# A new hand-written order and engine choice for the first 1086 recorded operations of a fused SSM-convolution and gMLP block

## The chip, the cores and the metric

The kernel runs on one core of a Trainium2 chip. A core has five engines that each work through their own instructions in order and wait for one another by semaphores: TensorE (PE in the profile), VectorE (DVE), ScalarE (ACT), GpSimd (POOL) and SyncE (SP), which here issues nearly all DMAs. The metric is the device time of one execution, in microseconds.

## The reference, cut to what matters

Batch 1, sequence S = 2048, width D = 640, F = 1728 with Fh = 864. Block A is a short convolution of `k` times `v`, a long convolution of the result with `ssm_k` by FFT, and a gate with the normalized input; block B is a gMLP that mixes along the sequence. Both are modulated by `silu(c) @ w_mod`.

```python
mod = (_silu(c) @ w_mod).reshape(c.shape[0], 6, 1, -1)     # sa, ca, ga, sb, cb, gb
h = _layernorm(x, axis=-1) * (1 + ca) + sa                 # x = A_q
# block A
k_shift = sum over 4 taps of k_pad[:, t:t+S, :] * shift_k[:, 3 - t]
kv = k_shift * v
y = irfft2(rfft2(kv padded to 2S) * rfft2(ssm_k padded to 2S))[:, :S]
y = y + kv * ssm_D
x = x + ga * (h * y)
# block B
h = _layernorm(x, axis=-1) * (1 + cb) + sb
z = gelu(h @ w_in)
z1, z2 = z[..., :Fh], _layernorm(z[..., Fh:], axis=-1)
g = einsum('ts,bsf->btf', w_sp, z2) + b_sp[None, :, None]
x = x + gb * ((z1 * g) @ w_out)
```

## The kernel before, in words

**What sets the order.** Everything up to the mix's first tile pair is recorded in a list of 1086 operations (class `Plan`); an operation is one closure that emits from one to some twenty instructions, or one DMA. The string `ORDER` (from L40) lists them as an engine letter and an operation number: P for PE, D for DVE, A for ACT, G for POOL, S for a DMA issued by SP. `Plan.run` emits them in that order. The letter decides which engine computes the operation where its closure allows more than one. Each engine then runs its own instructions strictly in the order in which the string names them, so an instruction whose input isn't there holds up all behind it on that engine. Tiles come from rotating pools; a tile's next user waits until the last reader of the buffer is through, so the list also sets how far one engine may run ahead of another. At most eight of SP's DMAs are under way at a time. Behind the plan, a plain loop over the tile pairs 1 to 7 and the last projection follow.

**The stages, by the names in the profile.**

- *Start.* `k` and `v` are brought in transposed by DMA (L521, into `big`), in halves for the first 128 channels. The four taps are matmuls of `big` with diagonal weights `dg` (built from `ident` and `sk` at L536 or L538, ahead of which `sk` is turned by PE), into the PSUM tile `sm`; DVE multiplies by `v` (L553) and SP writes the product `kv` to the DRAM scratch `kv_scr` (L559), from which it is read back in the order that the transform wants (L390, `X<-kv_scr`). `ssm_k` is read straight into `X` (L390); DVE adds `ssm_D` to its first row (L400). Tables of cosines are made: `T` (DVE, L343 and L345), `M` (ACT's sine at L348, the sign at L353, the negative at L356), `G` (PE flips of `M`, copies at L248, negatives at L375), `F1bd` (L255 and L300).
- *Transform, five groups u of 128 channels.* Stage 1 (`X` with `F1bd`, PSUM copied out by L248), then eight steps a group: forward matmuls into `pu` for `ssm_k` (copied to `KH` by ACT) and for `kv`; the **product** of the two by DVE (L462, 40 of these, into `Tf` or `T`); for half of the steps two sums into `W` (L476, by POOL or DVE); inverse matmuls into `pz`, copied to `Z` by ACT or DVE (L248). `Z` is turned by DMA (L685) or, for u = 4, by PE, and the last matmuls give `y`.
- *First norm and gate.* The statistics of the 16 token tiles of `xt` (loaded in four DMAs of four tiles, L566) are taken by ACT (L576, L577: two passes with accumulation, written to `gh`) or by DVE (L580, L581); L590 to L592 finish ACT's share; L606, L608 or L610 write the normalized `gh`. The gate (L661, L678, L746), the residual (L698) and the second norm's statistics (L704) come per group.
- *Second norm and first gMLP matmul.* In four groups g of four token tiles: variance (L829), `rstd` (POOL, L190 and L191), `nmr` (L833), the normalized tile `Z` (L843, L845 or L847). For g = 0 PE turns `Z` in two pieces (L858) and DVE or ACT modulate it (L871, L869); for g = 1 to 3 SP turns it by a DMA transpose (L889) and L895 or L897 modulate. Then come 64 **zz** groups, each of five matmuls of 432 columns into `pz` or `pu`; ACT's gelu (L920) writes each out, DVE takes statistics of one half (L926).
- *Mix.* Weight tiles `wT` (L974), sums `S` and `T` (L988, L998) and the products (L1013) of a Strassen-like scheme on pairs of token tiles; `w_o` (L1074, seven DMAs) and `bsp` (L1066, one DMA) are loaded for it. The first pair belongs to the plan.

Six groups of **fills** (L245 with `ident`, no useful result) keep PE at work in its first microseconds.

The lines that set the order:

```python
        for e, i in order:
            o = self.ops[i]
            assert e in o["eng"] and done.issuperset(o["deps"]), (e, i)
            ...
            o["fn"](engines[e])
            done.add(i)
```

Of the kernel before, what the change touches and what calls it, by code (L numbers as in the profile page):

```python
# [54 lines left out]
P313 A557 A314 P309 P331 A332 P61 D652 S94 D96 G298 D563 D564 G655 A310 P67 D62 P311 P375 D68 A312 P349 D350 P333 D334
P289 G597 D670 P73 A376 A558 A559 A560 P343 D344 P77 G598 P377 P317 A318 D129 A290 P277 A278 G335 D595 D596 A378 D653
G336 P323 A324 P299 D592 P337 A300 P319 A320 A338 G345 S71 D78 S599 G346 D74 D616 P379 A380 P369 G713 P600 G612 S69
P351 A352 P279 P347 D370 D601 P381 A382 P602 D280 D603 P365 P79 D366 D80 A348 G654 P604 P383 A384 S95 P399 A400 D605
P387 A388 P359 G281 G282 P283 A284 G371 G372 P401 A402 D360 P606 D607 G613 P353 D354 S97 P385 A386 D99 S580 D618 P403
A404 P75 P397 A398 P395 A396 D619 D671 P405 A406 P373 A374 P339 G361 G362 P363 A364 D615 P449 A450 G608 D76 P413 P367  # L60
A368 G355 D340 D414 P407 D408 P341 A342 G617 P453 G709 S620 P621 D622 G674 P393 D650 A454 P389 A394 A390 S81 G356 P623
D624 P451 A452 P439 D440 P357 A358 P625 D626 P391 A392 P455 P427 G409 G410 P627 P417 G609 P581 G673 G656 D428 G429
D430 A456 S98 P411 A412 D418 P471 A472 P473 D628 A474 D634 P431 P457 G419 G420 P443 P479 A458 D444 A480 D629 D632 P467
A468 P421 A432 P423 D424 G445 P475 A476 P433 D434 A582 S657 G639 A422 P415 G676 P461 A462 D631 P477 A478 D630 D638
P463 A464 P658 D659 A416 P465 A466 P441 A442 G446 P660 D635 P481 G435 P447 A448 P497 G710 D661 P662 G436 P437 A438
P425 A426 D482 D663 P664 D498 S583 P517 D518 G677 G483 G484 P485 A486 P507 D508 P499 P459 A460 P469 P501 A470 D665
G675 G519 G520 P521 A522 G509 G510 A500 A132 G708 P487 P584 D502 P513 D488 P511 A512 P491 P489 G503 A490 D514 P515
G504 D492 S678 G668 P505 P679 A516 A506 G493 D494 P495 A585 D633 D680 P681 D682 A496 P719 A720 D636 S586 P683 D684
P715 P721 A722 D716 P685 D686 D687 P717 A718 P587 A588 P723 P726 P725 G666 D691 G711 D689 D688 P724 D727 G714 G692
D728 D729 D758 D730 D759 G760 D690 D731 D732 D734 P735 P1037 D772 P1036 D761 A762 P749 D736 D750 D737 P589 S756 D741  # L70
D740 G763 P764 D766 D767 D768 S757 A590 G667 G610 D696 P765 A769 P742 D733 D738 D693 D834 D771 A770 D637 P794 G773
D695 D836 P812 P784 A795 A813 D751 D754 D774 P818 D837 P791 A775 D739 D694 D835 G697 D698 D776 P778 G838 A819 D839
A785 A840 D842 G843 P777 A782 A783 P787 A788 P816 A817 D780 G712 D841 P814 A815 D640 A792 D779 D781 P808 A809 D796
D752 P822 A823 S844 P820 A821 P824 A825 A846 P798 A848 D743 D789 D702 G669 D703 D706 G845 D744 D745 D746 D900 P801
D611 A799 D644 S1038 P805 A806 D793 P826 A802 A827 D641 D699 D901 D847 G849 P850 A851 D797 P857 P867 A868 D747 P892
A893 D643 D701 D755 D748 P882 D903 S1039 A883 D700 D642 D902 A858 P874 A875 D647 P880 G904 D905 D906 G908 D786 D907
D909 S910 D810 A881 P890 A891 P860 G915 A861 P864 A865 G911 P871 A872 P884 D1054 D1055 D1057 D705 D968 A912 D1056 D807
D811 G913 A885 D648 D704 D753 D645 D966 D646 D967 D969 G970 D866 P888 A889 S1040 D859 D862 D863 P886 A914 P878 A887
# [7 lines left out]
A1071 P1074 D1078 D1082 P1076 D1075 D1079 S1080 P1083 P1018 A1019 P1022 P1010 A1023 D1084 S1085 A1011 D1060 D1061
P1016 A1017 D1047 D1051 D1052 D1050
"""


# [1215 lines left out]
```

## Time and profile before

| | us |
|---|---|
| three runs | 308.17, 309.71, 309.59 |
| their median | 309.59 |
| the profiled execution | 310.85 |
| its span, first to last instruction | 309.1 |
| PE busy (share of the span) | 293.9 (95%) |
| DVE busy | 270.7 (88%) |
| POOL busy | 181.2 (59%) |
| ACT busy | 166.6 (54%) |

The span is what the rows of the profile add up to; 1.75 us lie around it in the profiled execution. That execution is 1.26 us above the median of the three runs. Where a row says `L580 DVE BATCH_NORM_STATS2 st<-xt 128x6 f32<-128x320 bf16 x16 | 6.9, 472 | 1.0 <-...`, it gives line, engine, operation, the tile written and the tile read with their partitions and elements, the count, the busy time of all in us, the mean of one in ns, and the engine's idle time just before them with what ended it. The granted TensorE clock is full in all 40 slices of the page. Rows of PE overlap a little, since the matmuls are pipelined and their ends are modelled.

### The profile page before, as it was taken

How to read it: one execution, taken by the hardware profiler on the slowest of the kernel's cores; microseconds unless marked ns; L12 is line 12 of the kernel's file. 1: busy time of each engine (PE TensorE's matmuls, PEld its weight loads, DVE VectorE, ACT ScalarE, POOL GpSimd, SP SyncE). 2: the span in 40 equal slices, each digit the busy share in tenths (PEclk: the TensorE clock that was granted, in tenths of full speed). 3: DMA queues.
4: the chain of work that ended last, by engine and by line, in shares of the span. 5: the costliest groups of instructions: out<-in, count | busy, mean ns of one | idle time of the engine just before them, and what ended most of it. 6: DMA issues, size and time to landing. Idle time of an engine off the chain costs nothing.

```text
span 309.1 us, 6509 instructions
## 1 busy us (share of the span) xinstructions
PE 293.9 (95%) x2485; PEld 195.3 (63%) x2485; DVE 270.7 (88%) x523; ACT 166.6 (54%) x302; POOL 181.2 (59%) x208
## 2 busy tenths in 40 slices
PE   7988989989999998989999999999999999999995
PEld 2765678867889998645555555555555555565554
DVE  8898998979998988998897998998999878888574
ACT  6988699978888957547676688141111111021110
POOL 2542877838988999555423612039858475673922
PEclk9999999999999999999999999999999999999999
DMA  8999899998995849404679910073477593730323
GB/s 177 210 227 253 231 305 224 220 190 196 225 223 113 203 84 298 152 2 95 127 146 237 204 3 0 2 127 70 89 152 165 120 192 73 167 81 21 83 55 111
DMA packets 127954, 45.23 MB, mean 146 GB/s; under 512 B 117071, under 2 KB 127156, under 8 KB 127924
## 3 DMA queue, kind: packets, MB, share of 16 engines
q1 hardware_dynamic: 127770, 44.78, 68.1%
q8 instruction: 19, 0.31, 0.4%
q14 instruction: 11, 0.09, 0.1%
q10 hardware_dynamic: 154, 0.05, 0.1%
HBM read 16.11 MB, written 5.24 MB: 69 GB/s over the span
## 4 chain that ended last, share of the span: by engine, by line
PE 47%; DVE 12%; issue 1%; POOL 1%; DMA 1%; ACT 1%; DVEq 0%; POOLq 0%
PE ps L1013 21%; PE pu L245 8%; PE pz L245 8%; PE po L1179 6%; DVE st L704 2%; PE pz L1013 1%; PE po L1140 1%; DVE Tf L462 1%; DMA uT<-u 1%; DVE T L462 1%; DVE xt L698 1%; PE pu L1013 1%; DVE u L1041 1%; DVE T L998 1%; DVE gh L746 1%
## 5 line engine op out<-in xcount | busy, mean ns | idle before, releaser
L245 PEld LDWEIGHTS <-Z 128*128 128x128 bf16 x320 | 31.2, 98 | 28.1 <-DVE Z L871 1.3
L245 PE MATMUL pu<-X,M 128*128 128x128 bf16 (+1 forms) x480 | 45.8, 237 | 2.3 <-DVE Tf L462 1.9
L245 PEld LDWEIGHTS <-M 128*128 128x128 bf16 x480 | 37.4, 98 | 8.8 <-issue 3.2
L476 POOL TENSOR_TENSOR W<-Tf 128x256 bf16<-128x256 f32 x47 | 34.7, 760 | 11.6 <-DVE Tf L462 8.3
L1013 PEld LDWEIGHTS <-S 128*128 128x128 bf16 x256 | 25.0, 98 | 21.6 <-issue 0.5
L245 PE MATMUL pz<-big,Z 128*128 128x432 bf16 x160 | 33.1, 346 | 0.8 <-DVE Z L871 0.8
L248 ACT CAST X<-s 128x1024 bf16<-128x1024 f32 x31 | 31.9, 1028 | 2.5 <-PE s L245 2.3
L245 PE MATMUL pu<-big,Z 128*128 128x432 bf16 x160 | 32.5, 346 | 0.0
L462 DVE TENSOR_TENSOR Tf<-pu,KH 128x1024 f32<-128x1024 f32 x25 | 30.3, 1219 | 2.4 <-PE pu L245 1.2
L1197 ACT COPY O<-po 128x320 f32<-128x320 f32 x7 | 3.0, 427 | 54.4 <-PE po L1179 54.4
L1013 PEld LDWEIGHTS <-wT 128*128 128x128 bf16 x192 | 18.8, 98 | 16.6 <-issue 1.0
L245 PEld LDWEIGHTS <-G 128*128 128x128 bf16 x330 | 24.7, 98 | 2.0 <-issue 0.2
L248 ACT CAST KH<-pu 128x512 bf16<-128x512 f32 x40 | 23.0, 600 | 5.1 <-PE pu L245 5.1
L248 ACT CAST Z<-pz 128x512 bf16<-128x512 f32 x38 | 22.3, 601 | 5.3 <-PE pz L245 5.1
L245 PEld LDWEIGHTS <-X 128*128 128x128 bf16 x288 | 18.1, 97 | 7.6 <-DMA X<-kv_scr 2.3
L1013 PE MATMUL ps<-X,wT 128*128 128x432 bf16 x112 | 22.7, 346 | 0.0
L1013 PE MATMUL ps<-T,S 128*128 128x432 bf16 x112 | 22.7, 346 | 0.0
L1200 POOL TENSOR_TENSOR O<-O,xt 128x320 f32<-128x320 f32 x7 | 6.4, 908 | 27.7 <-ACT O L1199 27.7
L1013 PE MATMUL ps<-X,S 128*128 128x432 bf16 x112 | 21.6, 346 | 0.0
L245 PE MATMUL s<-F1bd,X 128*128 128x256 bf16 x128 | 19.2, 272 | 2.2 <-DVE X L400 1.2
L245 PE MATMUL sm<-big,dg 128*128 128x512 bf16 (+1 forms) x80 | 20.4, 379 | 0.0
L926 DVE BATCH_NORM_STATS2 stz<-X 128x6 f32<-128x432 bf16 x32 | 18.1, 591 | 0.9 <-ACT X L920 0.7
(205 smaller groups left out, 664.3 us busy)
## 6 DMA issues: line engine op xcount, KB each, us to landing
wm<-in_w_mod_dram SPq DMA_DIRECT2D x6, 800.0 KB, 6.0
xt<-in_A_q_dram SPq DMA_DIRECT2D x4, 640.0 KB, 6.2
out_dram<-ot SPq DMA_DIRECT2D x15, 160.0 KB, 2.4
big<-in_B_w_in_dram SPq DMA_DIRECT2D x2, 1080.0 KB, 9.2
X<-in_A_ssm_k_dram SPq DMA_DIRECT2D x4, 512.0 KB, 5.2
kv_scr<-big SPq DMA_DIRECT2D x4, 512.0 KB, 3.5
X<-kv_scr SPq DMA_DIRECT2D x4, 512.0 KB, 4.8
w_o<-in_B_w_out_dram SPq DMA_DIRECT2D x6, 160.0 KB, 3.1
```

Of the source, the lines that this page charges most:

```text
L245: nc.tensor.matmul(o, lhsT=w, rhs=x, start=start, stop=stop)
L248: (e.copy if e is nc.scalar else e.tensor_copy)(dst, src)
L462: e.tensor_tensor(T_[:], (tl[pu] if src is None else tl[src])[:, :, :, None, :].to_broadcast(shape), tl[KH][:, :, None, :, :].to_broadcast ...
L476: e.tensor_tensor(tl[W][:, :, o, :], T_[:, :, 0, o, :], T_[:, :, 1, 1 - o, :], op=ALU.add if o else ALU.subtract)
L698: op("GD" if u < NU - 1 else "D", "res", lambda e: e.tensor_tensor(sl, sl, gl, op=ALU.add), r=[("gh", (u, g))], w=[("xt", (u, n)) for n in ...
L704: op("D", "ln2", lambda e, n=n: e.bn_stats(out=st2[:, n, (0, 0, 0, 1, 2)[u], :], in_=xt[:, n, us[0] * DU:(u + 1) * DU]), r=[("xt", (v, n)) ...
L746: op("D", "yml", lambda e, ghv=ghv, py=py, i0=i0, k=k: e.tensor_tensor(ghv, ghv, tl[py][:, i0:i0 + k], op=ALU.mult), r=[py], w=[("gh", (u, ...
L926: op("D", "stz", lambda e, i=i, n=n, fc=fc: e.bn_stats(out=stz[:, n, fc, :], in_=tl[z2][:, i, fc * FC:(fc + 1) * FC]), r=[(z2, (i, fc))], ...
L998: nc.vector.tensor_tensor(y if o is None else T[o][:, sl, :], x, y, op=ALU.subtract)
L1013: nc.tensor.matmul(ps[:, :FC], lhsT=lhs[:, s_, :], rhs=rhs(s_), start=(s_ == 0 and not more), stop=(s_ == HT - 1), skip_group_check=more)
L1179: nc.tensor.matmul(ps[:, :HS], lhsT=w(k), rhs=x(k), start=start and k == 0, stop=stop and k == n - 1, skip_group_check=True)
L1200: nc.gpsimd.tensor_tensor(m5, m5, x_of(1, 1), op=ALU.add)
```

## The change

Only the string `ORDER` is replaced; it is one line shorter, so that every line number behind it is one less than before (L248 becomes L247, and so on). The same 1086 operations stand in it. Twenty-six of them keep their place in the list. For 103 the engine letter changes: 26 from DVE to POOL, 25 from POOL to DVE, 23 from ACT to DVE, 17 from DVE to ACT, 7 from POOL to ACT and 5 from ACT to POOL. DVE then has 353 of the recorded operations (348 before), ACT 242 (246), POOL 125 (126), PE 305 and SP 61 as before.

```diff
 ORDER = """
-D0 D13 D100 G101 S88 A1 P1032 P7 A4 A10 G5 A23 D15 D102 D109 D103 D110 A112 D115 A111 S2 D6 P1033 P8 A11 D14 A16 D116
-A117 A118 D104 A105 S19 P1034 P26 A106 D90 D121 S82 D86 D17 D122 D18 G119 G113 P1035 P145 A146 P148 D149 S21 S83 D87
...
+S2 G101 D18 S524 A1 D0 D100 G5 P7 A4 A10 D102 S82 G103 D121 D122 D104 D115 A531 S19 D13 D14 S20 D6 S21 A16 P1033 D532
+A105 A106 S523 D15 A23 P1032 P8 P1035 S83 D11 P26 P24 S22 A533 D17 D116 D86 P1034 G107 G109 P145 A124 A146 P148 G108
...
 """
```

Three places show what moves. The first is ScalarE's start, before; `sk` holds the taps' coefficients, `dg` the first diagonal weights, `M_80` the table `M`, `f1c` the cosines for `F1bd`.

```order
L763 ACTIVATE warm<-warm 128x1
L248 COPY sk<-sm 128x4x5
L536 ACTIVATE dg<-ident,sk 128x128 x4
L348 ACTIVATE M_80<-T,mturn 128x4x64 x2
L248 CAST D_col<-sm 128x80
L255 ACTIVATE f1c<-f1i,mpi 128x32
L348 ACTIVATE M_80<-T,mturn 128x4x64 x4
```

The same place after the change:

```order
L762 ACTIVATE warm<-warm 128x1
L247 COPY sk<-sm 128x4x5
L575 ACTIVATE gh,sums<-xt 128x640
L576 ACTIVATE gh,sums<-xt 128x640
L254 ACTIVATE f1c<-f1i,mpi 128x32
L347 ACTIVATE M_80<-T,mturn 128x4x64 x2
L535 ACTIVATE dg<-ident,sk 128x128 x4
```

The two passes over the first token tile of `xt`, the cosines and two sines now stand ahead of the weights `dg`; the cast of `D_col` has gone to DVE.

The second place is SyncE's queue at the start, before:

```order
L390 DMA X<-in_A_ssm_k_dram 128x16x128
L754 DMA KH<-in_A_ssm_D_dram 80x8
L521 DMA_TRANSPOSE big<-in_A_k_dram 128x1024
L390 DMA X<-in_A_ssm_k_dram 128x8x128
L521 DMA_TRANSPOSE big<-in_A_v_dram 128x1024
L390 DMA X<-in_A_ssm_k_dram 128x8x128
L521 DMA_TRANSPOSE big<-in_A_k_dram 128x1024
L521 DMA_TRANSPOSE big<-in_A_v_dram 128x1024
L566 DMA xt<-in_A_q_dram 128x4x640
```

The same place after the change:

```order
L753 DMA KH<-in_A_ssm_D_dram 80x8
L565 DMA xt<-in_A_q_dram 128x4x640
L389 DMA X<-in_A_ssm_k_dram 128x8x128
L520 DMA_TRANSPOSE big<-in_A_k_dram 128x1024 x2
L520 DMA_TRANSPOSE big<-in_A_v_dram 128x1024
L565 DMA xt<-in_A_q_dram 128x4x640
L389 DMA X<-in_A_ssm_k_dram 128x8x128
L520 DMA_TRANSPOSE big<-in_A_v_dram 128x1024
L389 DMA X<-in_A_ssm_k_dram 128x16x128
```

A quarter of `xt` is now asked for ahead of all transposes and a second quarter between them, and the 16-row load of `X` (the second channel group of `ssm_k`), which was first, is ninth.

The third place is SyncE's queue around the turns of the gMLP's groups g = 1 to 3 (`Z<-Z`), before:

```order
L889 DMA_TRANSPOSE Z<-Z 128x20x128
L974 DMA_TRANSPOSE wT<-in_B_w_sp_dram 128x16x128 x2
L889 DMA_TRANSPOSE Z<-Z 128x20x128
L974 DMA_TRANSPOSE wT<-in_B_w_sp_dram 128x16x128
L1074 DMA w_o<-in_B_w_out_dram 128x640 x6
L1074 DMA w_o<-in_B_w_out_dram 96x640
L889 DMA_TRANSPOSE Z<-Z 128x20x128
```

The same place after the change:

```order
L888 DMA_TRANSPOSE Z<-Z 128x20x128
L973 DMA_TRANSPOSE wT<-in_B_w_sp_dram 128x16x128
L1073 DMA w_o<-in_B_w_out_dram 128x640 x6
L1073 DMA w_o<-in_B_w_out_dram 96x640
L1065 DMA bsp<-in_B_b_sp_dram 128x16x1
L973 DMA_TRANSPOSE wT<-in_B_w_sp_dram 128x16x128
L888 DMA_TRANSPOSE Z<-Z 128x20x128
```

The loads of `w_o` and `bsp` now stand ahead of the second turn instead of behind it.

More of the change, by code (lines that the diff above doesn't have):

```diff
@@ L86 @@
[L86 to L87 removed]
+S2 G101 D18 S524 A1 D0 D100 G5 P7 A4 A10 D102 S82 G103 D121 D122 D104 D115 A531 S19 D13 D14 S20 D6 S21 A16 P1033 D532
+A105 A106 S523 D15 A23 P1032 P8 P1035 S83 D11 P26 P24 S22 A533 D17 D116 D86 P1034 G107 G109 P145 A124 A146 P148 G108
+D25 D110 A118 A117 A111 A112 A123 G36 D27 A149 A147 S88 D127 P28 D150 D113 P30 D87 D31 P154 A114 D527 D125 G119 P151
@@ new lines @@
+A155 A156 D29 A152 G126 D153 P133 D528 A128 A534 D134 G48 P139 D120 P159 P161 A160 D90 A140 S32 P136 P157 P142 A162
+D529 P227 D137 P171 S34 A158 D530 A143 P163 D535 P39 A228 S33 A172 S35 P41 S84 G536 D138 A164 P167 S85 A168 P233 S46
+P173 D42 A175 D40 S47 P176 A174 D177 A178 P43 D537 D44 P179 G553 P182 P37 D181 D549 D38 P165 G72 A180 A184 S45 A183
+D141 G135 S526 P185 D186 A234 P229 G187 A166 P195 P211 G188 P49 P189 D196 P169 A230 D212 P231 A170 D50 P201 S3 D202
+P217 P53 D218 A232 G144 A190 G550 P203 A542 P191 S89 S525 G197 G551 A204 P9 A12 P205 G198 G213 D54 P55 A543 P251 D192
@@ new lines @@
+P51 P247 D56 G130 G131 A252 G214 D206 P253 D52 A248 P239 A254 S565 A240 D538 P221 P199 D222 P257 G554 P241 P566 S91
+A544 A200 D258 P568 P255 D539 P249 D256 P215 G223 D216 A242 G60 A545 A250 P193 G555 D93 P291 G224 S57 D292 S570 P225
+S58 A540 P237 A238 P301 G207 P269 A194 P235 S59 P219 A569 A567 P571 D541 A302 G208 D270 A236 G271 P573 D546 A226 D220
+D574 P307 P209 P245 G547 A552 P259 D572 D272 P67 D260 A308 P305 A246 P243 D548 D591 D561 D129 P265 A210 D68 G562 D261
+A306 A244 A557 P61 P285 D62 A563 G262 P303 P65 P263 S92 P63 A304 D286 P325 A564 D266 S94 A326 D66 P295 P273 D296 P275
@@ new lines @@
+P327 A264 D276 S575 G707 A274 D676 S70 P267 D64 D297 P321 A328 A322 G556 G558 D651 D649 P309 A310 G670 P329 D96 P315
+A330 S71 P576 P313 P331 P293 D559 D298 D577 A316 D597 S69 G287 P323 A314 D560 D595 S599 A332 P333 D598 D653 A324 G612
+D593 P77 G288 P375 P349 A268 P277 D334 A294 A376 D78 D350 G594 S95 P343 P377 A132 D344 G596 P578 P319 G709 A378 P299
+A278 P317 P73 D592 P379 D614 A320 A318 G335 A300 P311 P365 P289 D579 A380 G336 S97 G345 D616 A312 G652 P381 P337 D74
+D654 P600 D674 D346 P279 D366 D601 D280 A290 G615 P369 P602 D370 P79 P347 G281 A382 A338 G282 D603 D80 A348 P387 P399
@@ new lines @@
+G371 A388 P359 P604 G372 G710 D605 P353 P283 G618 A400 D360 P401 P606 A284 D354 G355 D99 P351 P339 D340 A402 P403 D711
+D607 A404 P383 D613 D619 P75 P385 A384 P405 P373 S580 A386 P395 D352 G361 G356 A406 G650 S620 A396 P397 P449 D362 A374
+A398 P407 D76 P367 P413 A450 G617 P363 S81 D408 A368 D414 P391 P453 D364 P621 D622 P389 A392 A454 P439 P357 G655 G677
+A390 P623 P451 A452 P427 D440 A358 D624 P341 G409 D428 P625 P417 G410 G611 G429 P455 D626 P411 P627 G430 S98 P443 P581
+A342 A456 D418 P471 A412 P473 D444 P431 A472 A474 P393 P423 D628 G419 D656 A394 A582 G420 P475 P441 P465 A476 P479 D424
@@ new lines @@
+D432 G672 D442 P433 S657 A466 P421 A480 P461 G609 G629 D434 P477 A422 D639 P425 P658 G445 P467 A462 G446 A478 D671 P517
+D659 A468 P447 A426 G435 P660 G436 D518 P457 A458 P437 A448 D661 P481 P463 G608 D482 P662 D663 G675 D631 G519 G520 G483
+G484 A438 A464 P415 S583 P507 A416 P664 P497 D508 P584 D498 P485 P459 A486 P521 G634 S678 A460 A522 P491 G509 P1037
+P501 D510 D633 A585 D492 P511 P487 D502 A512 G708 P499 A500 G493 G494 G503 P469 S586 G673 P495 D488 G504 S756 D665 P513
+A470 P489 D514 P679 A496 G667 D680 P515 G712 D630 G666 A490 D632 P681 P505 A516 D682 P683 D637 D684 A506 P715 P719 A720
@@ new lines @@
+P805 A825 D640 D746 A806 D751 D786 D700 P801 G702 A823 P820 D790 D900 D642 D699 A848 D902 D701 S1038 D849 D754 D704
+D641 P818 A821 D748 P798 D847 D901 D755 G846 A802 D753 G845 S1045 A819 D645 D903 D706 S1044 D647 P874 G904 D646 D905
+P867 P850 A799 A875 D705 D793 D796 P860 D648 P857 A851 D969 A868 A858 S1039 P864 D967 D703 P882 A861 D752 G906 P880
+D859 A865 P886 A881 A883 G909 P853 D1053 D1049 D966 G907 D968 P884 A854 D862 D807 P892 G908 D800 P871 A885 D810 S910
+D803 A887 A872 D912 P890 D863 D876 P888 G911 P878 A913 D873 A891 A915 D914 A889 A879 P916 A893 G970 S1041 P923 D797
@@ new lines @@
+P940 D1054 D971 A972 A917 G975 D811 D974 D804 A941 P926 D869 D855 P919 A927 D866 P952 A920 D852 P933 P954 D856 S1040
+D870 D1055 D1052 A953 A924 D1058 D918 P937 G973 D1059 S976 D978 G828 P930 A979 A934 D1050 D928 A938 G977 D980 D925 A981
+D829 A955 D942 D877 D833 D921 A931 D831 P958 G894 S1043 P982 P996 P1006 A983 D932 A959 A830 A832 D922 A1007 D935 D939
+D943 D1057 D936 D895 P999 P1003 D1056 A1000 P992 D929 A1004 A997 P950 A993 A951 P948 D994 D898 D1005 A897 A896 P946
+D1001 P1018 A949 P985 D998 D1062 G960 A947 D1002 D899 D1008 P989 A1019 A986 P956 D961 P1024 P1012 A964 D963 D962 D1009
@@ L88 @@
+A990 D987 A965 D991 P1014 D995 D984 A957 D988 A1025 A1013 G1026 A1015 D1051 P944 D1066 P1070 D1027 A945 D1063 A1030
+P1020 A1029 S1042 D1064 P1072 A1071 D1028 A1021 D1031 D1065 P1074 D1068 D1067 P1077 D1075 P1081 P1022 A1073 P1076 D1069
+D1078 D1082 D1079 P1083 S1080 P1010 P1016 A1017 D1084 A1011 S1085 D1047 A1023 D1061 D1046 D1048 D1060
 """
```

48 lines of the change are left out of this document (5 added, 43 removed).

## The prediction, made before the changed kernel ran

> **What bounds the kernel now.** I read the page's head first, then the busy time of the engines in six stretches that I cut at events of the timeline: 28.2 is the start of the first product (L462), 120.2 the end of the last, 134.1 the end of DVE's last modulation of the first piece of g = 0 (L871), 142.7 that of the second piece, 204.8 the start of the mix's loop behind the plan.
>
> ```profile
> span 309.1 us, 6509 instructions
> PE 293.9 (95%) x2485; PEld 195.3 (63%) x2485; DVE 270.7 (88%) x523; ACT 166.6 (54%) x302; POOL 181.2 (59%) x208
> core 0: us, PE busy (x) PEld busy (x) DVE busy (x) ACT busy (x) POOL busy (x), PEclk, DMA share, GB/s
> 0.00:28.20 28.20, 24.98 (x190) 15.66 (x191) 23.75 (x71) 23.18 (x48) 9.24 (x23) 1.00 1.10 215
> 28.20:120.20 92.00, 87.56 (x1080) 74.93 (x1078) 85.44 (x127) 77.11 (x133) 73.66 (x85) 1.00 0.93 204
> 120.20:134.10 13.90, 11.79 (x235) 9.35 (x232) 12.73 (x33) 7.26 (x12) 9.90 (x10) 1.00 0.50 181
> 134.10:142.70 8.60, 8.04 (x50) 4.27 (x50) 7.55 (x26) 5.14 (x10) 5.50 (x8) 1.00 0.00 0
> 142.70:204.80 62.10, 61.84 (x339) 33.06 (x339) 56.50 (x140) 39.62 (x73) 17.80 (x23) 1.00 0.55 107
> 204.80:309.10 104.30, 99.64 (x601) 58.07 (x599) 84.70 (x131) 14.30 (x29) 65.09 (x60) 1.00 0.52 108
> ```
>
> The reader is to see that DVE idles 4.45, 6.56, 1.17 and 1.05 us in the first four stretches (length less busy), 13.2 of 142.7 us, and that PE idles 0.26 in the fifth. So two engines take turns as the bound: DVE up to 142.7, then PE, which from there has a fixed amount of work. The chain that ended last says the same; these are three of its pieces, with start, length and what ran.
>
> ```profile
> 119.00 1.14 DVE Tf L462
> ...
> 138.79 0.43 DVE Z L847
> ...
> 144.67 2.74 PE pu L245 x15
> ```
>
> It lies mostly on DVE through the products to L847, then mostly on PE. In the 15 matmuls of the third row are three zz groups of five: 0.91 us a group. Since nothing is added or removed, the time changes only by (a) when DVE is through with the second piece, which is DVE's work to there plus its idle time, and (b) what PE still has to do then, plus its waits. Everything behind 204.8 is code that the change leaves alone, and stays at 104.3.
>
> **Stretch 1, to the first product.** Ahead of it the new order gives DVE one more token tile's statistics, the finish of ACT's share (in two runs of three instructions where one run stood later), a normalized tile, two signs and one negative of `M`, one more negative of `G` and the cast of `D_col`; it takes away four passes over `T`, the diagonal weights, one copy of `G` and one of `X`. The rows (busy, mean ns of one):
>
> ```profile
> L580 DVE BATCH_NORM_STATS2 st<-xt 128x6 f32<-128x320 bf16 x16 | 6.9, 472 | 1.0 <-DMA xt<-in_A_q_dram 1.0
> L591 DVE TENSOR_TENSOR sums<-mv 128x4 f32<-128x4 f32 x2 | 1.3, 631 | 0.1
> L610 DVE TENSOR_SCALAR gh<-xt,mv,rstd 128x640 bf16<-128x640 bf16 x4 | 2.3, 599 | 0.0
> L353 POOL TENSOR_SCALAR M<-M,sgn 128x512 bf16<-128x512 bf16 x4 | 2.8, 695 | 8.9 <-ACT X L248 7.1 <-ACT M L348 1.9
> L375 DVE TENSOR_SCALAR G<-G 128x1024 bf16<-128x1024 bf16 x1 | 0.4, 373 | 0.0
> L343 DVE TENSOR_SCALAR T<-KH,mstep 128x256 f32<-128x256 f32 x8 | 2.4, 346 | 0.0
> L538 DVE TENSOR_TENSOR dg<-ident,sk 128x512 bf16<-128x512 bf16 x1 | 0.7, 684 | 0.0
> L248 DVE COPY G<-sm 128x1024 bf16<-128x1024 bf16 x3 | 1.9, 667 | 0.0
> ```
>
> In: statistics 2 x 0.47 and about 0.2 for their aggregate; the finish, 0.63 for one instruction of its three, at 1.6 for one run of them; 0.60; 0.37; 0.2 for the cast. A sign or negative of `M` on DVE stands in no row: half of L375's 0.37 (half the elements) from below, the 0.70 of POOL from above; I take 0.37, nearest to the row of DVE, so 1.1 for three (0.6 to 2.1). Sum 5.0. Out: 4 x 0.35, 0.68, 0.67 and 0.68 for the copy of `X`, 3.4. That is +1.6, and as the finish has six instructions instead of three, up to +3.1; I take **+2.1**.
>
> The idle time changes too, since the start of the convolution moves. Before:
>
> ```profile
> 4.03 1.28 ACT L536 ACTIVATE dg<-ident,sk 128x128 bf16<-128x128 bf16 x4
> 5.21 0.89 ACT L348 ACTIVATE M<-T,mturn 128x256 bf16<-128x256 f32 x2
> 6.93 1.03 PE L245 MATMUL sm<-big,dg 128*128 128x512 bf16 x4
> L576 ACT ACTIVATE gh<-xt 128x640 bf16<-128x640 bf16 x8 | 5.9, 738 | 2.5 <-DMA xt<-in_A_q_dram 2.5
> xt<-in_A_q_dram SPq DMA_DIRECT2D x4, 640.0 KB, 6.2
> X<-in_A_ssm_k_dram SPq DMA_DIRECT2D x1, 512.0 KB, 4.1
> ```
>
> The weights `dg` were through at 5.3, the first taps ran at 6.93. Now ACT first waits for `xt`, whose DMA is SP's second, issued about 2 us in; at the median of 6.2 from issue to landing it lands near 8.2, at the 4.1 of the 512 KB load of `ssm_k` in the first microseconds near 6.2. Then come 2 x 0.74 for the passes, 0.3 for the cosines, 0.89 for two sines and 1.28 for `dg`: 4.0 us, so the first taps start at 10.2 to 12.2 instead of 6.93. All else in the conv's first half, and ACT's copies of stage 1, queue behind. From the first multiplication by `v` to the first product DVE then has 17.4 us of work by the new order. With taps at 11.5, 1.0 for them and 1.2 of small waits (2.7 us of such waits stood behind 12 us before; the 1.0 for `xt` goes) the first product starts at 11.5 + 1.0 + 17.4 + 1.2 = **31.1, +2.9** (range +1.5, where DVE fills the early gap, to +4.5).
>
> [...]
>
> **Stretch 2, the products.** Here DVE takes five more sums and four more copies to `Z`:
>
> ```profile
> L476 DVE TENSOR_TENSOR W<-Tf 128x256 bf16<-128x256 f32 x3 | 1.3, 441 | 0.1
> L248 DVE CAST Z<-pz 128x512 bf16<-128x512 f32 x2 | 1.4, 676 | 0.0
> DVE X L400 <- DMA X<-in_A_ssm_k_dram: 1.9, 1, 1.9
> DVE Tf L462 <- PE pu L245: 1.2, 3, 0.8
> DVE Tf L462 <- ACT KH L248: 0.7, 1, 0.7
> ```
>
> 5 x 0.44 + 4 x 0.68 = 4.9. Against that, what was put ahead of the first product leaves (statistics, finish, tile, about 3.2), and three small statistics and a residual go behind the last product (1.2): +0.5, work 86.0. Of the 6.56 us idle, 1.9 waited for the second group's `ssm_k` (third row); in the new order that addition stands later in DVE's program than its DMA needs, so it goes. The rest are waits for PE and ACT. In the new order DVE has 2.6 us more to do up to the last product (2.1 + 0.5), PE the same matmuls but for one fill, so PE and the copies are further ahead; I let that take about half, 1.2, of the remaining 4.7. Idle **3.5**, from 1.0 (only the gaps between instructions) to 6.5 (other stalls come in place of the old). The stretch: 86.0 + 3.5 = 89.5 (92.0 before), last product through at 31.1 + 89.5 = **120.6** (120.2 before).
>
> **Stretches 3 and 4, to the second piece.** A sum and a residual leave, an extra PE-side copy comes: 12.7 becomes 11.8. In the fourth, three normalized tiles of g = 1 go behind the last modulation (3 x 0.45) and a product of `y` and a residual come in: 7.55 becomes 8.1. Work 19.9, idle 2.0 of the 2.2 before: 21.9. Last modulation of the second piece at **142.5** (142.7).
>
> **Stretch 5, PE.** It has 57 zz groups left instead of 56: 61.84 + 0.91 = 62.75. A new wait is likely in front of g = 1. Before:
>
> ```profile
> 140.12 0.16 DVE L833 SCALAR_TENSOR_TENSOR nmr<-mv,rstd 128x4 f32<-128x4 f32 x1 [0.91 <-POOL rstd L191]
> 141.71 3.08 SPq L889 DMA_TRANSPOSE Z<-Z  x1
> 147.65 1.52 ACT L895 ACTIVATE Z<-Z,sb_col,cb_col 128x512 bf16<-128x512 bf16 x2 [0.58 <-DMA Z<-Z]
> 147.76 1.67 POOL L897 TENSOR_SCALAR Z<-Z,cb_col,sb_col 128x512 bf16<-128x512 bf16 x2 [4.02 <-DMA Z<-Z]
> ```
>
> The tiles of g = 1 were ready at 141.6, the turn landed at 147.6 and was modulated by 149.4; from L833 that is 9.3 us, and L833 came 2.4 us ahead of the last modulation. In the new order L833 of g = 1 stands behind it. The g = 1 input is then there some 9.2 us after the last modulation, and PE has about nine groups, 8.2 us, until then: a wait of **1.0** (0 to 1.9). Stretch 5 is 63.75, its end at 142.5 + 63.75 = 206.25.
>
> **Sum.** 206.25 + 104.3 = 310.55, 1.45 above the span of before. The profiled execution (310.85) lay 1.26 above the median; I add the difference to the median: 309.59 + 1.45 = **311.0**.
>
> **Rivals.**
>
> - *DVE closes its gaps (faster).* The early gap is filled (+1.5 instead of +2.9), the idle time of stretch 2 falls to 1 to 2 (-1.5 to -2.5) and g = 1 arrives in time (-1.0): -3.9 to -4.9 together, 306.1 to 307.1; with one of them missing up to 308.2. For it: 13.2 us of idle DVE are there to be taken, and much of it follows from the order alone. Against it: PE was itself busy 87.56 us in that stretch, and two engines that feed each other would both have to run at 97% and more.
> - *The start is lost in full (slower).* The place is ACT's wait for `xt` ahead of `dg`. If `xt`, four more loads and transposes share the DMA engines (already 1.10 busy by the first row of the stretches), taps start at 12.2 or later, the first product at 32.7 (+4.5), and stretch 2 idles as before for half the rest: +1.6 and +1.5, 314.1. It decides once `xt` lands behind 8 us. For it: nothing on ACT can pass that wait. Against: DVE has tables to make meanwhile.
> - *The second turn comes late (slower).* Before, SP issued it at 155.13 and the seven loads of `w_o` afterwards:
>
> ```profile
> 155.13 3.33 SPq L889 DMA_TRANSPOSE Z<-Z  x1
> 160.62 3.47 SPq L1074 DMA_DIRECT2D w_o<-in_B_w_out_dram  x7
> ```
>
>   Now those 3.5 us and `bsp` stand ahead of one `wT` and the turn: issue at 159 to 160.5, g = 2 ready 7.7 us later, against PE's need at about 166.5. Price 0 to 3 us, up to 314.0.
> - *The order makes no difference.* Both lists keep DVE and then PE at the same work: 309.6.
>
> A mechanism of its own, small: the first fills of before ran cold.
>
> ```profile
> 3.70 2.74 PE L245 MATMUL s<-ident 128*128 128x512 bf16 x6
> 9.10 1.02 PE L245 MATMUL sm<-big,dg 128*128 128x512 bf16 x4
> ```
>
> Six took 2.74 (0.47 apart), later ones 1.02 for four (0.21 apart). If PE stands idle for 2 to 4 us between fills and taps and falls back, eight taps and stage-1 matmuls lose 0.26 each, 2.1 us of PE, mostly beside DVE's own work: at most 312.5. [...]
>
> **How the numbers follow.** Forecast 0.42 (309.4 to 312.5), gaps closed 0.30, start lost 0.13, late turn 0.08, no difference 0.04, cold PE 0.03. A measurement of this kernel can tell about 0.5% (1.55 us) from no change: 308.04 to 311.14. Of the forecast's 0.42 about 0.24 lie inside, 0.16 above and 0.02 below; of the gaps-closed case 0.25 below and 0.05 inside; of the slower ones 0.23 above, 0.01 inside; no difference is inside. Faster 0.27, same 0.34, slower 0.39. The range, 306.6 to 314.2, leaves out the far ends of both sides.
>
> **What would show it.** First taps later than 10 us and the first product at 29.7 to 32.7; DVE busy near 25.9 and 86 us in the first two stretches; no wait of L399 for `ssm_k` in the second; a wait of PE for L894 or L896 ahead of the first zz of g = 1; the second turn issued after 159. I would be wrong most easily in the idle time of stretch 2, the only large term that no row gives.

## The result, and the profile after

| | before | after |
|---|---|---|
| median of the runs | 309.67 us (10 runs, 308.17 to 311.29) | 311.96 us (10 runs, 310.99 to 313.41) |
| profiled execution, span | 310.85, 309.1 | 311.84, 309.7 |
| median span of all runs | 308.1 (19 later runs) | 309.85 |
| time around the span | 1.78 | 2.12 |

The ratio is 1.0072, with a 95% interval of 1.0044 to 1.0099: slower by about 0.7%. Two things in this table matter for the reading. The profiled execution of before lies 1.0 us above the median span of 19 later runs of that kernel, so the two traces show only 0.6 of the 1.75 us by which the spans differ. And 0.34 us of the loss lie outside the span, where no row is.

First the page of the changed kernel: span, busy time by engine, and the chain that ended last.

```profile
span 309.7 us, 6534 instructions
...
PE 295.1 (95%) x2485; PEld 195.4 (63%) x2485; DVE 272.4 (88%) x532; ACT 164.1 (53%) x298; POOL 186.2 (60%) x209
...
PE 40%; DVE 6%; DMA 4%; SPq 4%; POOL 2%; issue 1%; ACT 0%; DVEq 0%; ACTq 0%
```

PE's busy time is 1.2 longer for the same matmuls; the slow taps of the first microseconds, shown below, are about as much. DVE's share of the chain has halved, from 12% to 6%. The next view is the busy time in stretches, cut at the same events as before: first product, last product, end of the second piece, start of the loop over tile pairs, end of its first pair (behind its first four `po` from `V`), end.

```profile
core 0: us, PE busy (x) PEld busy (x) DVE busy (x) ACT busy (x) POOL busy (x), PEclk, DMA share, GB/s
0.00:31.70 31.70, 25.61 (x173) 14.75 (x174) 25.37 (x80) 24.76 (x53) 16.34 (x28) 0.95 0.98 208
31.70:121.70 90.00, 89.32 (x1100) 76.19 (x1098) 87.63 (x130) 73.52 (x125) 69.33 (x81) 1.00 0.89 202
121.70:133.50 11.80, 10.48 (x227) 9.01 (x227) 11.40 (x34) 5.43 (x9) 8.84 (x11) 1.00 0.59 212
133.50:139.40 5.90, 5.89 (x40) 3.43 (x41) 5.90 (x24) 4.01 (x9) 5.36 (x7) 1.00 0.01 1
139.40:203.80 64.40, 63.92 (x349) 33.90 (x348) 53.87 (x140) 41.05 (x75) 21.34 (x26) 1.00 0.50 100
203.80:223.90 20.10, 18.26 (x106) 10.23 (x105) 19.37 (x23) 4.48 (x9) 16.09 (x12) 1.00 0.48 92
223.90:309.70 85.80, 81.63 (x498) 47.90 (x495) 68.89 (x111) 10.81 (x22) 48.85 (x49) 1.00 0.52 112
```

The last two stretches of before, which the prediction took as one, are these:

```profile
204.60:223.30 18.70, 18.26 (x106) 10.25 (x105) 17.33 (x22) 3.65 (x7) 16.24 (x12) 1.00 0.52 91
223.30:309.10 85.80, 81.58 (x497) 47.93 (x495) 67.57 (x110) 10.83 (x22) 48.85 (x49) 1.00 0.53 112
```

From the end of the first pair on, both take 85.8. Ahead of it, after less before: +3.5 to the first product, -1.9 over the products, -4.8 to the second piece, +2.4 for PE's stretch behind it and +1.4 in the first pair, 0.6 together. The change loses at the start, wins more than that back by 139.4 (3.2 us ahead of before), and then gives it all back, since PE is what counts: it has 58 zz groups left instead of 56, and the first pair has a new gap in PE (20.1 less 18.26 busy; before 0.44).

PE counts even earlier than that. Over the products it idles 0.68 us of 90.0 in the changed kernel (before, 4.44 of 91.9), and from the first product to the loop 2.5 of 172.1 (before, 7.4 of 176.4). A wait that is taken from DVE there can hardly make the changed kernel faster.

The 3.2 us of lead are in part the one execution that was profiled. The kernel g4, below, has the order of before up to the second piece, and its profile reaches that point at 140.9 and not at 142.6: its products take 90.5 us, and its wait for `ssm_k` is 1.1 us and not 1.9. Against that profile the changed kernel is 1.5 us ahead.

Where the waits went, by engine (us in total, times, longest), PE over the whole span first:

```profile
PE sm L244 <- DMA KH<-in_A_shift_k_dram: 2.2, 1, 2.2
PE ps L1012 <- DVE c L1038: 1.5, 2, 0.8
PE po L1178 <- DVE ot L1216: 1.1, 1, 1.1
PE sm L244 <- DVE KH L764: 0.9, 1, 0.9
...
PE sm L244 <- ACT dg L535: 0.7, 1, 0.7
```

and DVE:

```profile
DVE Z L896 <- DMA Z<-Z: 3.5, 2, 1.9
DVE big L552 <- PE sm L244: 3.5, 4, 1.9
...
DVE bcol L1080 <- DMA bsp<-in_B_b_sp_dram: 2.4, 1, 2.4
...
DVE T L344 <- POOL T L342: 1.0, 1, 1.0
```

DVE's wait for `ssm_k` (1.9) is gone, and no wait ahead of a product is over 0.4 now. New or longer are DVE's waits for the first taps, for `bsp` and for the turned tiles, and PE's waits for DVE in the loop's first pair: 1.1 for `ot` and one of the two 0.8 for `c`. The start on ACT and PE:

```profile
5.64 0.74 ACT L575 ACTIVATE gh<-xt 128x640 bf16<-128x640 bf16 x1 [2.74 <-DMA xt<-in_A_q_dram]
...
8.69 1.26 ACT L535 ACTIVATE dg<-ident,sk 128x128 bf16<-128x128 bf16 x4
```

```profile
9.13 3.16 PE L244 MATMUL sm<-big,dg 128*128 128x512 bf16 x8 [0.70 <-ACT dg L535]
...
14.08 1.89 PE L244 MATMUL sm<-big,dg 128*128 128x512 bf16 x8
```

ACT stands 2.74 us waiting for `xt`, and PE waits for `dg` behind it. The first eight tap matmuls take 3.16 us, the next eight 1.89: the granted clock of TensorE was 0.50 to 0.54 for most of the first eight. The clock by the microsecond, in windows with the columns of above (PEclk is the third number from the end):

```profile
9.00:10.00 1.00, 0.87 (x3) 0.29 (x3) 1.00 (x3) 1.00 (x5) 1.00 (x1) 1.00 1.02 204
10.00:11.00 1.00, 1.00 (x4) 0.42 (x4) 0.41 (x1) 0.97 (x3) 1.00 (x2) 0.54 0.80 221
11.00:12.00 1.00, 1.00 (x4) 0.30 (x2) 0.00 (x0) 0.93 (x3) 1.00 (x2) 0.50 1.08 348
12.00:13.00 1.00, 1.00 (x4) 0.36 (x3) 0.68 (x2) 0.00 (x0) 1.00 (x2) 0.50 1.19 292
13.00:14.00 1.00, 1.00 (x9) 0.80 (x8) 1.00 (x3) 0.40 (x1) 1.00 (x2) 0.76 1.37 135
```

### The profile page after: what moved, and what is told of

It reads as the page before. It is cut to its first block, busy times and chain, and to the rows that moved or that the text cites. A ratio compares the mean times of both kernels' runs of the same rounds, so it can differ in the third digit from the quotient of the medians.

```text
span 309.7 us, 6534 instructions
## 1 busy us (share of the span) xinstructions
PE 295.1 (95%) x2485; PEld 195.4 (63%) x2485; DVE 272.4 (88%) x532; ACT 164.1 (53%) x298; POOL 186.2 (60%) x209
## 4 chain that ended last, share of the span: by engine, by line
PE 40%; DVE 6%; DMA 4%; SPq 4%; POOL 2%; issue 1%; ACT 0%; DVEq 0%; ACTq 0%
PE ps L1012 20%; PE po L1178 7%; PE pu L244 4%; PE pz L244 4%; DMA Z<-Z 3%; SPq L973 2%; PE pz L1012 2%; PE pu L1012 1%; DVE S L987 1%; PE po L1139 1%; SPq L1073 1%; DMA uT<-u 1%; POOL Z L844 1%; DVE V L1160 1%; POOL xt L697 1%
## 5 line engine op out<-in xcount | busy, mean ns | idle before, releaser
L475 POOL TENSOR_TENSOR W<-Tf 128x256 bf16<-128x256 f32 x43 | 31.3, 745 | 12.7 <-DVE Tf L461 5.0
L244 PE MATMUL pu<-big,Z 128*128 128x432 bf16 x160 | 33.6, 346 | 0.5 <-ACT M L919 0.4
L244 PE MATMUL pz<-big,Z 128*128 128x432 bf16 x160 | 32.6, 346 | 0.1
L247 ACT CAST X<-s 128x1024 bf16<-128x1024 f32 x30 | 30.7, 1024 | 3.5 <-PE s L244 3.4
L247 ACT CAST KH<-pu 128x512 bf16<-128x512 f32 x40 | 23.5, 598 | 6.0 <-PE pu L244 6.0
L247 ACT CAST Z<-pz 128x512 bf16<-128x512 f32 x34 | 19.9, 599 | 8.2 <-PE pz L244 8.1
L244 PE MATMUL sm<-big,dg 128*128 128x512 bf16 (+1 forms) x80 | 21.3, 395 | 0.7 <-ACT dg L535 0.7
L244 PEld LDWEIGHTS <-X 128*128 128x128 bf16 x288 | 18.2, 97 | 5.2 <-issue 1.4
```

The costliest lines, as they stand in the source:

```text
L244: nc.tensor.matmul(o, lhsT=w, rhs=x, start=start, stop=stop)
L247: (e.copy if e is nc.scalar else e.tensor_copy)(dst, src)
L475: e.tensor_tensor(tl[W][:, :, o, :], T_[:, :, 0, o, :], T_[:, :, 1, 1 - o, :], op=ALU.add if o else ALU.subtract)
```

## The experiments

Two theories at first. **START**: the loss is made ahead of the first product, by ACT's wait for `xt` ahead of `dg` and by the cold TensorE. **TAIL**: it is made behind the second piece, where DVE waits for `bsp` and comes late to the mix. All times of events in this table are from each kernel's one profiled execution (us); the ratio is against runs of before on the same chip, with its 95% interval.

| kernel | median | ratio | first taps | first product | last product | second piece | loop starts | first pair ends |
|---|---|---|---|---|---|---|---|---|
| before | 309.67 | 1 | 6.9 | 28.2 | 120.1 | 142.6 | 204.6 | 223.3 |
| after | 311.96 | 1.0072 (1.0044 to 1.0099) | 9.1 | 31.7 | 121.7 | 139.4 | 203.8 | 223.9 |
| g1_start_only | 317.94 | 1.0271 (1.0240 to 1.0303) | 9.1 | 32.2 | 127.8 | 150.2 | 212.2 | 230.9 |
| g2_all_but_start | 315.67 | 1.0189 (1.0154 to 1.0225) | 7.3 | 28.1 | 125.9 | 143.6 | 207.6 | 227.8 |
| g3_all_but_tail | 311.44 | 1.0053 (1.0024 to 1.0081) | 9.1 | 31.6 | 121.7 | 139.4 | 205.7 | 224.3 |
| g4_tail_only | 310.49 | 1.0021 (1.0002 to 1.0041) | 6.7 | 28.0 | 118.5 | 140.9 | 203.0 | 223.2 |
| e5_dg_first | 311.23 | 1.0046 (1.0027 to 1.0066) | 8.7 | 31.2 | 121.4 | 139.1 | 202.7 | 222.9 |
| e6_bcol_late | 311.97 | 1.0055 (1.0033 to 1.0077) | 9.1 | 32.6 | 122.6 | 140.3 | 204.2 | 224.4 |
| e8_fills | 311.88 | 1.0053 (1.0034 to 1.0072) | 9.3 | 31.7 | 121.8 | 139.8 | 204.0 | 224.1 |
| e9_reserve | 311.10 | 1.0046 (1.0029 to 1.0062) | 9.1 | 31.4 | 121.5 | 139.2 | 205.0 | 223.2 |
| e10_dg_dwide | 312.13 | 1.0075 (1.0051 to 1.0100) | 7.5 | 31.4 | 121.6 | 139.3 | 204.4 | 224.6 |
| e11_three_moves | 312.23 | 1.0082 (1.0053 to 1.0110) | 7.7 | 32.1 | 122.5 | 140.3 | 206.2 | 224.4 |
| e12_before_xt_first | 311.87 | 1.0069 (1.0030 to 1.0108) | 9.6 | 31.6 | 122.6 | 145.1 | 207.1 | 225.8 |
| e13_before_addD_late | 310.40 | 1.0035 (1.0009 to 1.0062) | 7.3 | 28.1 | 119.1 | 141.6 | 203.6 | 222.2 |

**Grafts of the two orders.** Each takes one order with its engines up to a cut, and what is left in the other order. For g1 and g2 the cut is the first product, for g3 and g4 the end of the second piece:

```diff
-<order of before>
+g1: after up to D186, then before      g2: before up to D186, then after
+g3: after up to D781, then before      g4: before up to D781, then after
```

> The changed order and engines up to the first product (D186), the order and engines of before for all that is left. Theory START (the loss is made ahead of the first product: ACT's wait for xt ahead of the weights dg, cold TensorE, and it is not won back): +1.5 to +3 us against before, first product near 31.7, time less span near 2.1. Theory TAIL (the loss is made behind the second piece of g = 0, where VectorE waits for bsp and is late at the mix): the start is made up for on the way, -0.5 to +0.7 us.

> The order and engines of before up to the first product, those of the change for all that is left. START: 0 to -2.5 us against before, first product near 28.2, time less span near 1.75. TAIL: +1 to +2.5 us, with the wait of VectorE for bsp (2.4 us) still there.

> The changed order and engines up to the last modulation of the second piece of g = 0 (D781), those of before for all that is left. START: the loss stays, +1.5 to +3 us against before. TAIL: it goes, -2 to +0.3 us, with no wait of VectorE for bsp and the first tile pair of the mix's loop 18.7 us long as before.

> The order and engines of before up to D781, those of the change for all that is left. START: within 0.7 us of before. TAIL: +1.5 to +3 us, with the wait for bsp and a first tile pair of the mix's loop of about 20 us.

g1 and g2 are 2.7% and 1.9% slower and say nothing of the two parts: at the first product the orders are too far apart, and the seam makes waits that neither kernel has. The waits of DVE in g1, then of PE in g2, longest first:

```profile
DVE Tf L462 <- PE pu L245: 8.3, 6, 4.9
```

```profile
PE pz L245 <- POOL W L476: 7.4, 1, 7.4
```

g4 has a clean seam: between its second piece and the loop PE does not idle at all, so that its 0.21%, 0.6 us, can be put down to the order behind the second piece. The seam of g3 is not clean. PE idles 2.3 us there, against 0.5 in the changed kernel and 0.3 in the kernel before, mostly in waits for ACT's gelu. The longest of them:

```profile
PE pu L245 <- ACT X L920: 1.3, 1, 1.3
```

So g3's 0.53% (1.6 us) holds some 1.8 us of waits that the graft made, and is no price of the order up to the second piece. That 0.53% and 0.21% add up to about the 0.72% of the whole is chance: the 0.34 us outside the span, too, stand in neither of the two. What is left for the order up to the second piece is a difference, 1.75 less 0.6, so about 1.15 us of span; no run measures it. By the bands written down both times fit START, each at the edge (+1.56 and +0.61 us), but the first pair comes out as TAIL expected: in g4 it takes 20.2 us, as in the changed kernel; in g3 18.6, as before (windows with the columns of above):

```profile
203.00:223.20 20.20, 18.36 (x107) 10.26 (x106) 19.47 (x23) 4.48 (x9) 16.16 (x12) 1.00 0.48 95
```

```profile
205.70:224.30 18.60, 18.17 (x106) 10.20 (x105) 17.21 (x22) 3.60 (x7) 16.21 (x12) 1.00 0.57 92
```

DVE's wait for `bsp` stands in neither of them, so g4 has the tail's loss without that wait.

**The tail: bsp, or too few groups in reserve.** The order behind the second piece also differs in what PE does behind the last product of the mix's first pair. PE in before, then after, in order of time:

```profile
200.77 2.90 PE L245 MATMUL pu<-big,Z 128*128 128x432 bf16 x15
203.51 1.08 PE L245 MATMUL pz<-big,Z 128*128 128x432 bf16 x5
```

```profile
201.77 1.08 PE L244 MATMUL pu<-big,Z 128*128 128x432 bf16 x5
202.69 1.08 PE L244 MATMUL pz<-big,Z 128*128 128x432 bf16 x5
```

Four zz groups (3.65 us) stood there and covered DVE's last sums for the pair; the change leaves two. e6 takes the wait away, e9 puts two groups back; both are moves in the changed order:

```diff
 e6_bcol_late
-... D1053 ... P1072 A1071 ...
+... P1072 D1053 A1071 ...
 e9_reserve
-... P1070 ... P1020 ... A1021 ... P1022 ... P1083 S1080 P1010 P1016 A1017 ...
+... P1070 ... P1083 P1020 P1022 S1080 P1010 P1016 A1021 A1017 ...
```

> The changed kernel, with VectorE's bcol (D1053, it waits 2.4 us for bsp) moved back to just ahead of its first user. Theory BSP (that wait makes VectorE late at the mix and is the tail's +0.6 us): 0.5 to 1.0 us less than the changed kernel, first tile pair of the loop 18.7 to 19.3 us in place of 20.1. Rival RESERVE (VectorE is behind TensorE there anyway and makes the wait up; what counts is how many zz groups stand behind the last product of the first pair): within 0.3 us of the changed kernel, the pair still 20.1.

> The changed kernel, with two zz groups (P1020, P1022, and the gelu of the first) moved behind the last product of the mix's first pair, so that four groups stand there as before, in place of two. RESERVE: products of the pair end 1.8 us earlier, VectorE's sums too, the first tile pair of the loop takes 18.7 to 19.2 us in place of 20.1, 0.5 to 1.2 us less than the changed kernel. BSP: within 0.3 us.

e6: the wait is gone, and nothing else gets better: 311.97, the pair from 204.2 to 224.4. So the longest new wait on DVE costs nothing that these runs can tell, as the rival RESERVE expected. e9: the pair takes 18.2 us, and PE idles 0.05 us in it:

```profile
205.00:223.20 18.20, 18.15 (x106) 10.25 (x105) 17.47 (x20) 4.49 (x9) 16.62 (x12) 1.00 0.50 98
```

and the median is 0.86 below the changed kernel's. That is the size expected of the theory RESERVE, though the intervals of the two ratios overlap. Of the 1.9 us that the pair gains, 1.3 are lost ahead of it: between second piece and loop PE idles 1.8, and 0.5 in the changed kernel's profile. Two waits, 0.5 where the first of the moved groups stood and 0.3 ahead of their new place, are the price of the move. The longest wait is not:

```profile
PE pz L245 <- POOL Z L897: 1.0, 1, 1.0
```

It stands at 149 us, some 40 us ahead of anything that e9 moves, where PE wants the turned tiles of g = 1. e10 and e11 have it too (0.94 and 0.57), and the changed kernel's own profile does not, though the order from the first product to there is the same in all four. So one execution loses up to 1 us there, and another nothing. The gap in the first pair is shown; its worth, 0.6 us by g4 and 0.9 by e9, is less sure.

**The start.** Three moves in the changed kernel, and one in the kernel before:

```diff
 e5_dg_first
-... D104 D115 A531 S19 ... D15 A23 P1032 ...
+... D104 D115 A23 A531 S19 ... D15 P1032 ...
 e8_fills
-FILLS = (4, 6, 2, 2, 4, 3, )
+FILLS = (6, 6, 2, 5, 4, 3, )
 e10_dg_dwide: e5 and
-... D121 D122 D104 D115 ... S20 D6 S21 ...
+... D121 D122 D6 D104 D115 ... S20 S21 ...
 e12_before_xt_first (the order of before)
-... S88 A1 ... G5 A23 ... S524 A531 A532 ...
+... S88 S524 A1 ... G5 A531 A23 ... A532 ...
```

> The changed kernel, with ACT's first diagonal weights (A23) moved ahead of the first passes over xt (A531); nothing else. Theory ACT QUEUE (the head's +1.6 us comes from ACT's wait for xt ahead of dg, by late taps and a cold TensorE behind them): first taps near 7 in place of 9.13, granted clock 1.00 from 9 to 14 us, 1.0 to 1.8 us less than the changed kernel, +0.1 to +0.4% against before. Rival SP QUEUE (xt ahead of the transposes makes k itself late): taps no earlier than 8.5, within 0.4 us of the changed kernel.

> The changed kernel, with five more fill matmuls (two ahead of the wait for KH, three ahead of the wait for dg), so that TensorE has no gap up to the taps; the order is untouched. If the half clock from 10.1 to 13.6 us is a loss of the whole kernel: granted clock 1.00 from 9 to 14 us and 0.5 to 1.3 us less than the changed kernel. If VectorE has other work meanwhile and sets the pace: clock 1.00 and within 0.3 us.

> The changed kernel with dg (A23) ahead of the passes over xt, as in e5, and VectorE's cast of KH (D6, L764, which TensorE's turn ahead of the taps waits for) moved from behind two steps on T to ahead of the one that waits for POOL. If the rest of the head's loss is this second wait ahead of the taps: first taps near 7.5 instead of e5's 8.67, another 0.4 to 0.8 us less than e5's 311.23. If VectorE sets the pace by then: within 0.3 us of e5.

> The kernel before, with one DMA (a quarter of xt, S524) moved from behind the third transposes to second on SP, and ACT's passes over its first tile (A531) moved ahead of dg (A23); nothing else. ACT QUEUE: first taps at 8.5 to 10 in place of 6.93 and +0.7 to +1.8 us. If stretch 2 takes it up: within 0.4 us.

e12 has the clearest effect: one DMA and one ACT operation moved in the kernel before cost 0.69%, 2.3 us of mean and 1.95 of median span, with the first product 3.4 later, about as much as in the changed kernel (3.5). Its ACT and PE rows, and DVE's new waits:

```profile
7.53 0.74 ACT L576 ACTIVATE gh<-xt 128x640 bf16<-128x640 bf16 x1 [3.54 <-DMA xt<-in_A_q_dram]
```

```profile
9.57 1.89 PE L245 MATMUL sm<-big,dg 128*128 128x512 bf16 x4 [0.30 <-ACT dg L536]
```

```profile
DVE KH L765 <- DMA KH<-in_A_ssm_D_dram: 2.6, 1, 2.6
...
DVE X L400 <- ACT D_col L248: 1.7, 1, 1.7
```

So in the kernel before, `xt` first is enough by itself to make such a loss: by `KH`, whose DMA stands behind the 640 KB there (DVE waits 2.6 us for it), and by what queues on ACT behind the passes (DVE waits 1.7 us for `D_col`). It does not show that the changed kernel loses in the same way. There SP asks for `KH` ahead of `xt` and DVE makes `D_col`, and neither of these two waits of DVE is in its trace; DVE waits for the taps (3.2 us) and for `T` (1.0). In the changed kernel, undoing the move in part does not win the loss back. e5 gives 0.7 us of median (the intervals of the ratios overlap), with taps only 0.5 earlier, since PE's turn ahead of them waits for `KH` (7.80, in e5 as after). e10 removes that wait too. The taps then run at 7.47, and yet the first product stands at 31.4, and the median is the changed kernel's. DVE's waits up to there in e10:

```profile
DVE T L345 <- POOL T L343: 2.6, 2, 1.7
DVE big L553 <- PE sm L245: 0.8, 2, 0.5
```

DVE now waits for the passes over `T` that the change gave to POOL. With the taps 1.7 us earlier, the first product is only 0.3 earlier, so the taps alone do not set 31.7. That DVE's longer work (25.4 us before the first product, 25.9 in e10) and its waits for POOL set it is what the traces suggest; no run gives the passes over `T` back to DVE. e8 shows that the cold TensorE does not set it: with five more fills eight taps take 1.98 instead of 3.16, the first product stays at 31.7, the time at 311.88. The half clock falls into time in which PE would have idled: in e9, whose eight taps took 2.13 us, PE idles 7.6 us ahead of a first product at 31.4, in the changed kernel 6.1. e10 is no better than e5, and rather worse; its PE idles 1.3 us between second piece and loop, e5's 0.1. Most of that, 0.94, is the wait for the turned tiles of g = 1 named above. Why those tiles come later in one execution than in another is open.

**All moves together.** The edit is that of e10 and e9.

> The moves of e10 and of e9 (dg first, KH's cast early, two zz groups kept behind the last product of the first pair). If start and tail add up: 1.6 to 2.4 us less than the changed kernel, 309.5 to 310.4, within 0.3% of before. If they share a bound: no better than 310.7.

The gains do not add up: 312.23, no better than the changed kernel, though the first pair's gap is gone here too (PE idles 0.05 in it). The first product stands at 32.1, and PE idles 1.6 us between second piece and loop. What single moves gain at one place, TensorE or DVE loses at the next wait.

**The stall that the change removes.** One move in the kernel before:

```diff
-... S94 D96 G298 D563 D564 G655 A310 P67 D62 P311 ...
+... S94 G298 D563 D564 G655 A310 P67 D62 D96 P311 ...
```

> The kernel before, with one VectorE operation moved three VectorE places later: the addition of ssm_D to the fourth channel group (D96, it waits 0.9 to 1.9 us for its DMA in every profile with the middle of before) behind two normalized tiles and a multiplication by v. This is the one stall of stretch 2 that the change removes by itself. If VectorE's idle time sets the end: the wait goes and 0.5 to 1.5 us less than before, a kernel faster than both. If the wait comes back as another (TensorE feeding stage 1 late): within 0.4 us.

The wait for `ssm_k` is gone from the trace, and the first pair ends 1.1 us earlier than in the profile of before, but that is the slow profile named above. g4 keeps the wait (1.1 us) in the same order up to there and has the last product at 118.5 and the second piece at 140.9, earlier than e13's 119.1 and 141.6. And the runs of e13 are 0.35% slower, not faster (12 runs, 309.78 to 312.52; the profiled one, 309.81, is nearly the fastest of them). So no kernel here beats the one before, and this stall is not worth its length. What slows the median is open: one trace of a fast execution can't show it.

## Why the prediction came out as it did

The forecast was 311.0, a little slower, with 306.6 to 314.2; 311.96 was measured. The direction was right, and ACT's wait for `xt`, the late taps and the lost time at the start came as forecast. The premise that DVE bounds the kernel up to the second piece did not hold, the terms were off by more than the total, and that the sum is as close as it is owes something to luck, since they partly cancel.

- **First product, +2.9 forecast, +3.5 measured.** The rows gave +1.6 of DVE work and I took +2.1; DVE was busy 25.37 instead of 23.75, +1.6. The rest, 1.9, is idle time (I had 0.8). The taps came at 9.13, not 10.2 to 12.2, because `xt` landed by 5.6 and not at 6.2 to 8.2. By e10 the taps alone are not what sets 31.7.
- **Stretch 2, 89.5 forecast, 90.0 measured.** DVE's work was 87.6 against 86.0, its idle time 2.4 against 3.5, so the two errors nearly cancel. The wait for `ssm_k` went as forecast, but e13 shows that its going is worth less than the 1.9 that I credited, and in g4's profile it is only 1.1 long. I had held against the rival of closed gaps that both engines would have to run at 97% and more: in this stretch they did (PE 99%, DVE 97%). The rival still failed: the early gap was not filled, and what DVE won behind it PE, now saturated, could not use.
- **Stretches 3 and 4, 21.9 forecast, 17.7 measured.** This term was mis-sized most. Work was 17.3, not 19.9, and idle 0.4, not 2.0. Of the 2.6 us of work, 1.7 are in two groups whose durations I carried over: the five residuals (L698 before, L697 after) took 543 ns in the mean before and 367 after, and L833's three instructions of 364 became two of 152, with no wait for `rstd`. One residual of 1.35 us and one `nmr` of 0.83 make up most of it. Both are as long in the profiles of g1, g4, e12 and e13, which have the order of before there, and in the profile of before each starts within 0.4 us of a residual on POOL. So they belong to the order and not to one execution, but what makes them long is not shown.

```profile
L698 DVE TENSOR_TENSOR xt<-xt,gh 128x512 bf16<-128x512 bf16 (+1 forms) x5 | 2.7, 543 | 0.1
...
L833 DVE SCALAR_TENSOR_TENSOR nmr<-mv,rstd 128x2 f32<-128x2 f32 (+1 forms) x3 | 1.1, 364 | 0.9 <-POOL rstd L191 0.9
```

```profile
L697 DVE TENSOR_TENSOR xt<-xt,gh 128x512 bf16<-128x512 bf16 (+1 forms) x5 | 1.8, 367 | 0.1
...
L832 DVE SCALAR_TENSOR_TENSOR nmr<-mv,rstd 128x2 f32<-128x2 f32 x2 | 0.3, 152 | 0.0
```

- **Stretch 5, 63.75 forecast, 64.4 measured.** The 1.0 of waiting ahead of g = 1 did not come in this profile, though it did in those of e9, e10 and e11 (0.98, 0.94 and 0.57); instead 58 groups were left, not 57, since DVE came earlier than PE could use. The premise "DVE bounds up to 142.7" fails from the first product on: PE idles only 0.7 us from there to 121.7 and another 1.3 to 139.4. Of DVE's 3.2 us lead 0.8 were left when the loop began.
- **"Everything behind 204.8 stays at 104.3" failed.** It became 105.9. The code is the same, but it starts with DVE behind PE, as two zz groups in reserve do not cover what four did. I had counted the work ahead of the loop, not the order at its end. g4 and e9 show this step.
- **The second turn**, a rival at 0 to 3 us, was issued at 156.58, not behind 159. The chain that ended last does run over SP and the turned tiles from 141 to 173 us (SPq and DMA 4% each on the page), but PE idles only 0.48 us in all of stretch 5, so that its price in this execution is at most that.
- **The cold TensorE** happened, 1.2 us of PE, and e8 shows it hidden, as that paragraph said it mostly would be.
- **The base.** I added the difference of spans to the median of before. By spans of all runs the change is +1.75, not the +0.6 of the two profiles, and 0.34 more lies outside the span. That +1.45, forecast for what is 0.6 in the two profiles, comes so close to the 1.75 of all runs is luck.

## What to carry to other kernels

When an order is changed, give each stretch to the engine that will bound it afterwards: a lead of an engine that hands over to a saturated one is lost at the seam (here 0.8 of 3.2 us were left). Look at the last few instructions ahead of unchanged code, and at what covers the other engines there. And put nothing on an engine's queue that waits for a large load ahead of a small step that the start of another engine needs (ACT stood 2.74 us for `xt` ahead of `dg`); read differences below 2 us off a single profile with care: two profiles of one and the same order up to the second piece reach it at 140.9 and 142.6.

## What was not expected of the hardware

- TensorE went to a granted clock of 0.50 for about 3.4 us (10.1 to 13.5) although no wait of it between its first matmul at 2.20 and there was over 0.9 us; between 6.9 and 9.1 it was busy for 0.6 of 2.2 us. Five kernels have this start unchanged: in four the eight taps took 3.09 to 3.43 us, in e9 2.13, so it is a matter of chance as well as of order. What sets it is not shown.
- The granted clock of the rows does not show every slow phase. In e12 four taps took 1.89 us and in e5 eight took 3.09, both at a granted clock of 1.00; there only the spacing of the matmuls, 0.47 and 0.39 us, tells of it (0.25 for the eight taps of e8).
- The time around the span is 2.10 to 2.18 us in the seven kernels that have the changed order throughout, but for single moves, 2.00 in g2, and 1.77 to 1.80 in all others. No row shows what it is; it wasn't settled.
